# A gated recurrence followed by a gated linear unit on one core: square roots in batches of four chunks, decay constants by a series, and a new hand-written order of all queues

## The chip, the cores and the metric

The kernel runs on one core of a Trainium2 chip. The metric is the device time in microseconds (us) of one launch; a measurement is the median of several runs. Beside the timed runs there is a profile: one execution of the program, taken by the hardware profiler. The engines are named as in the profile: PE (TensorE, matmul), PEld (its weight loads), DVE (VectorE), ACT (ScalarE), POOL (GpSimd), SP (SyncE, which issues nearly all the DMAs).

## The reference

All inputs are float32. `x`, `r_gate` and `i_gate` have the shape 4 x 6336 x 256. The first half is a gated recurrence along the sequence, the second a gated linear unit with a causal convolution of five taps:

```python
log_a = 8.0 * sigmoid(r_gate) * log(clip(sigmoid(a_param), 1e-6, 1 - 1e-6))
a_t   = exp(log_a)
norm  = sqrt(maximum(1.0 - a_t * a_t, 1e-6))
h_t   = a_t * h_(t-1) + norm * sigmoid(i_gate) * x        # y_t = h_t, h = 0 at the start of each sequence
gate  = sigmoid(sum over k < 5 of conv_w[k] * y[t - 4 + k])
out   = (gate * (y @ w_val)) @ w_out
```

## The kernel before

The four sequences are laid end to end as 25,344 time steps. They are cut into 51 windows (`w`, mostly 512 steps) and 28 chunks (`c`): chunks 0 and 1 have 256 steps, chunk 2 has 512, chunks 3 to 25 have 1024 (two windows each), chunk 26 has 512 and chunk 27 has 256. For a window, the three inputs and the output are 512 KB each (256 KB for the windows of 256 steps).

One chunk passes through these steps; each step is a function named by two letters, and the number behind it is the window or the chunk:

- `lr`, `li`, `lx` (line 278): SP issues the loads of `r`, `i` and `x` of a window into rings of four windows each.
- `ta`, `tb` (lines 296 and 299): ACT takes the tanh of half of `r` and `i`, a chunk at a time (a sigmoid is half of 1 + tanh).
- `tr` (343): PE transposes the result for `r`, half of the channels (`h` = 0, 1) at a time, so that channels lie on the partitions. Where GROUPS names two chunks together, one `tr` covers both.
- `ex` (359): ACT takes the exponential with the decay constant `khf` as scale and bias, which gives `a`, into a ring `aring` of 5120 steps, that is five chunks of 1024.
- `sq` (367, POOL) squares `a` into a second ring of the same length, `ering`; `sa` (375) is the same on ACT.
- `rt` (386): ACT takes the square root for a whole batch of chunks (BATCHES). Exp and tanh lie in one of ACT's table sets and the square root in another, so a table load (line 518) is issued wherever the list passes from one kind to the other. Where the chunks of a batch do not lie end to end in the ring, the root is taken in pieces.
- `pp`, `up` (306 and 318, POOL), or `xp` and `uv` (323, PE and 332, DVE): (1 + tanh) times `x`.
- `nt` (401, PE) transposes the roots back, `xg` (408, DVE) multiplies them in, `xt` (417, PE) transposes the product, `sc` (439, DVE) is the scan over time, one half of the channels at a time.
- `cv` (451, PE) is the convolution of a window, `tg` (458, ACT) its tanh, `vl` (466, PE) the product with `w_val`, `gv` (471, DVE) the gating, `ou` (481, PE) the product with `w_out`, `cd` (489, DVE) or `ca` (491, ACT) the copy out of PSUM, and `st` (502, SP) the store.

The string `ORDER` is the order of all this work, written out: one word for each step, with the PSUM banks behind an `@`. The loop at the end of the kernel goes through the words and issues each step's instructions, so that each engine gets, in its own queue, the subsequence of the words that belong to it. An engine works through its queue in order and waits, at the head, for what the instruction needs. Words that stand together in the list run at about the same time: PE's `cv.45`, the first matmuls that the list names behind `rt.9`, start at 265.50 us, and `rt.9` at 265.45 us. Before the loop stand five set-up words, among them `s_kt` (lines 225 to 235), which computes the decay constant `khf` = 4 log(clip(sigmoid(a_param))) on 128 x 2 numbers.

The recurrence ties the rings together: chunk `c + 5` lies where chunk `c` lay in `aring`, so its `ex` waits for `sc` of chunk `c`.

Of the kernel before, what the change touches and what calls it, by code (L numbers as in the profile page):

```python
# [8 lines left out]
P = 128  # L9
CONV_K = 5  # L10
FP32 = mybir.dt.float32
# [7 lines left out]
BATCHES = [[0, 1, 2], [3, 4], [5, 6, 7], [8, 9, 10], [11, 12, 13], [14, 15, 16], [17, 18, 19], [20, 21, 22], [23, 24, 25],  # L19
    [26, 27]]  # L20
# [3 lines left out]
NU = 10  # L24
# [7 lines left out]
GROUPS = [[0], [1], [2], [3, 4], [5, 6], [7, 8], [9, 10], [11], [12], [13, 14], [15, 16], [17, 18], [19, 20], [21], [22],  # L32
# [3 lines left out]
s_ident s_small s_kt s_diag lr.0 ta.0 tr.0.1@0 lr.1 ta.1 lr.2 ta.2 ex.0.1 tr.1.1@1 ex.1.1 tr.1.0@2 tr.2.0@3 ex.1.0  # L36
ex.2.0 tr.0.0@0 tr.2.1@4 lr.3 lr.4 ex.0.0 sq.0.1 sq.0.0 ta.3 lr.5 lr.6 ta.4 sq.2.0 tr.3.1@0,1 li.2 lx.2 tb.2 ex.2.1
li.0 sq.1.0 s_wl.1 tb.0 lx.0 li.1 sq.1.1 ex.3.1 sq.3.1 sq.4.1 lr.7 tb.1 pp.1 tr.3.0@2,3 ex.3.0 sq.4.0 xp.0@4 uv.0 lr.9
lr.10 ta.6 xp.2@0,1 lr.8 sq.3.0 li.4 li.3 ta.5 tb.3 sq.2.1 s_wl.3 lx.1 lx.4 xp.4@2,3 lx.3 rt.0 uv.2 lx.6 li.6 s_wl.2
s_wl.0 lr.13 up.1 li.5 li.8 nt.0@0 xg.0 nt.2@1 nt.1@0 li.7 uv.4 xt.0@5,4 pp.3 up.3 lx.5 lx.7 lr.14 lr.12 rt.1 xg.1  # L40
xg.2 sc.0.1 sc.0.0 nt.3@6,7 xg.3 tb.4 li.10 lx.8 lr.11 li.9 xt.2@0,1 tr.5.0@2,3 xt.1@4,5 ex.5.0 cv.0@6,7 tg.0 sc.1.1
tb.5 li.12 sc.1.0 xt.3@5,4 sc.2.1 cv.1@6,7 tr.5.1@2,3 tg.1 ex.5.1 sc.2.0 cv.2@0,1 xp.7@6,7 sc.3.0 sc.3.1 s_wcast
vl.1@2,3 gv.1 pp.6 pp.5 vl.0@4,5 up.6 lx.10 up.5 pp.8 gv.0 nt.4@2,3 ou.0.0@4 ou.1.0@5 uv.7 tg.2 ta.8 cd.1.0 sq.6.1
lx.9 li.11 cd.0.0 st.1 st.0 ta.7 up.8 tb.6 tr.7.1@0,1 ex.7.1 xg.4 tr.7.0@6,7 ex.7.0 tb.7 lx.11 vl.2@4,5 gv.2 lr.16
lx.12 li.13 xt.4@2,3 sc.4.1 cv.3@0,1 sq.6.0 sq.5.0 sq.5.1 tg.3 vl.3@4,5 xp.9@6,7 sc.4.0 sq.7.1 sq.7.0 rt.2 lr.15 lr.18
gv.3 pp.10 sq.8.1 uv.9 vl.5@0,1 ou.3.0@4,5 ou.2.0@2,3 cd.3.0 cd.2.0 li.14 lr.17 st.3 lx.13 xp.11@6,7 cv.5@2,3 uv.11
tg.5 st.2 up.10 lx.14 li.15 li.16 pp.12 nt.5@6,7 xg.5 tb.8 li.17 up.12 lx.16 li.18 ta.10 gv.5 ta.9 lr.20 cv.6@4,5
nt.6@2,3 xg.6 nt.7@6,7 sq.8.0 xg.7 xt.5@0,1 cv.4@2,3 tg.4 tg.6 sc.5.0 tr.9.0@6,7 ex.9.0 vl.4@2,3 sc.5.1 gv.4
tr.9.1@4,5 ex.9.1 tb.9 pp.13 up.13 lx.17 lx.15 pp.14 up.14 lx.18 ou.5.0@0,1 cd.5.0 ou.4.0@2,3 cd.4.0 st.5 st.4 li.20
lr.19 sq.10.0 sq.9.0 sq.9.1 sq.10.1 xt.6@6,7 sc.6.1 sc.6.0 vl.6@4,5 gv.6 tb.10 li.22 pp.17 pp.15 pp.16 pp.18 cv.7@2,3  # L50
vl.7@0,1 tg.7 rt.3 xt.7@2,3 gv.7 li.21 up.18 up.17 lr.21 lr.22 cv.9@6,7 ou.6.0@4,5 cd.6.0 ou.7.0@0,1 cd.7.0 up.16
cv.10@4,5 tg.10 cv.8@0,1 st.7 li.19 lx.21 sc.7.1 sc.7.0 vl.9@4,5 tg.9 gv.9 st.6 vl.10@6,7 gv.10 ta.11 lr.23 tg.8
nt.8@2,3 xg.8 lx.22 up.15 tb.12 ou.9.0@4,5 cd.9.0 vl.8@0,1 gv.8 nt.9@6,7 tr.11.1@2 pp.22 xg.9 pp.21 up.21 xt.8@4,5
sc.8.0 ta.12 lr.24 li.26 tb.11 pp.20 pp.19 cv.12@0,1 tg.12 tr.12.1@3 ex.11.1 ex.12.1 sq.12.1 ou.8.0@6,7 cd.8.0
cv.11@0,1 tg.11 tr.12.0@4 tr.11.0@2 up.22 ex.11.0 nt.10@6,7 lr.26 lr.25 sc.8.1 vl.11@0,1 gv.11 xt.9@3,2 sc.9.1 li.25
ta.13 ex.12.0 lx.19 sq.11.1 sq.11.0 up.19 ou.11.0@0,1 cd.11.0 cv.14@4,5 li.23 lx.20 st.8 li.24 ta.14 tg.14 tb.14
vl.12@0,1 up.20 sc.9.0 tr.13.0@4,5 ex.13.0 tr.13.1@2,3 xg.10 ou.10.0@6,7 xt.10@4,5 gv.12 ou.12.0@0,1 ex.13.1 cd.10.0
tb.13 cv.13@6,7 tg.13 st.11 st.9 cv.15@2,3 tg.15 sq.13.0 sq.13.1 lx.25 lr.29 sq.12.0 rt.4 lr.28 st.10 pp.26 pp.23
lx.24 lr.27 sc.10.0 cd.12.0 sc.10.1 vl.14@6,7 vl.13@0,1 gv.13 lr.30 sq.14.0 gv.14 vl.15@2,3 gv.15 cv.17@4,5 st.12
# [490 lines left out]
```

## Time and profile before

| what | value |
|---|---|
| timed runs | 294.39 us median (293.57, 294.39, 295.06) |
| profiled execution, span from first to last instruction | 291.5 us |
| median less that span | 2.9 us |
| busy in the span: ACT, DVE, PE, POOL | 275.0, 247.3, 243.8, 233.0 us |
| moved by DMA | 104.35 MB on SP's queue |
| table loads on ACT | 20 (18 on line 518, one each on lines 186 and 234), 1.28 us each |
| first root of batch 0, of batch 2, of batch 9 (the last) | 28.89, 59.62, 265.45 us |
| end of the last matmul, and of the last copy | 287.5, 288.2 us |

No device time is listed for the profiled execution itself: its span is what is known of it, and the timed median lies 2.9 us above it.

Busy time of an engine is not its share of the blame: the span has a start in which little is loaded yet, a long middle in which all engines run at once, and an end in which the inputs are already consumed. The profile is read stage by stage, and the chain of waits says which engine ended last in each.

### The profile page before, as it was taken

The numbers are of one execution on the slowest core, as the hardware profiler recorded it, in microseconds if no ns is written. First come the engines' busy times: TensorE is split into PE (matmuls) and PEld (weight loads), VectorE is DVE, ScalarE is ACT, GpSimd is POOL, SyncE is SP. The second block draws the span as 40 slices with busy tenths as digits, with TensorE's granted clock in tenths as the row PEclk, the third lists the DMA queues.
The fourth block names the chain that finished last, engine by engine and source line by source line (L and its number), as shares of the span: only waits on it lengthen the run. The fifth ranks groups of instructions, "written<-read, shape, count | busy, mean of one in ns | idle before, by whom it ended". The sixth has DMA issues, their size and how long they took to land.

```text
span 291.5 us, 6283 instructions
## 1 busy us (share of the span) xinstructions
PE 243.8 (84%) x2509; PEld 167.6 (57%) x2509; DVE 247.3 (85%) x206; ACT 275.0 (94%) x198; POOL 233.0 (80%) x155
## 2 busy tenths in 40 slices
PE   2281798997986988989888988899889998999993
PEld 1141475455744766567656666657457765767662
DVE  2030589988999999999999999999999999999891
ACT  7799989999999999999999999999999999999563
POOL 1449789999899899999996599998998799976000
PEclk9996789999999999999999999999999999999999
DMA  7999999999999999999999999999999958983354
GB/s 243 356 409 388 386 408 413 338 419 414 408 417 398 388 393 400 386 347 415 412 398 384 409 410 371 411 339 386 408 414 421 413 211 322 338 329 128 147 217 181
DMA packets 29996, 104.75 MB, mean 359 GB/s; under 512 B 3335, under 2 KB 3854, under 8 KB 29966
## 3 DMA queue, kind: packets, MB, share of 16 engines
q1 hardware_dynamic: 29952, 104.35, 92.6%
q8 instruction: 19, 0.31, 0.4%
q14 instruction: 11, 0.09, 0.1%
q10 hardware_dynamic: 14, 0.01, 0.0%
HBM read 78.39 MB, written 25.95 MB: 358 GB/s over the span
## 4 chain that ended last, share of the span: by engine, by line
ACT 39%; PE 18%; DMA 17%; DVE 12%; issue 12%; SPq 1%; ACTq 0%; DVEq 0%
ACT tbring L299 9%; DMA iring<-in_i_gate_dram 8%; DMA rring<-in_r_gate_dram 8%; ACT ering L386 8%; ACT tgring L458 7%; ACT taring L296 6%; DVE yring L439 5%; PE banks L481 5%; PE banks L451 4%; ACT L518 4%; PE banks L466 3%; ACT aring L359 3%; PE banks L401 3%; DVE oring L489 2%; DVE tgring L471 2%
## 5 line engine op out<-in xcount | busy, mean ns | idle before, releaser
L367 POOL TENSOR_TENSOR ering<-aring 128x1024 f32<-128x1024 f32 (+2 forms) x54 | 91.9, 1723 | 21.4 <-ACT aring L359 21.4
L439 DVE TENSOR_TENSOR_SCAN yring<-aring,yring,banks 128x1024 bf16<-128x1024 f32 (+5 forms) x54 | 105.9, 1988 | 1.3 <-PE banks L417 1.2
L318 POOL TENSOR_TENSOR uring<-tbring,xring 128x1024 bf16<-128x1024 bf16 (+1 forms) x45 | 94.5, 2112 | 3.0 <-PE banks L481 1.3
L451 PE MATMUL banks<-yring,diag 64*64 64x512 bf16 (+7 forms) x1080 | 62.2, 361 | 3.0 <-DVE oring L489 1.7
L471 DVE SCALAR_TENSOR_TENSOR tgring<-tgring,banks 128x1024 bf16<-128x1024 bf16 (+1 forms) x51 | 59.1, 1179 | 5.3 <-PE banks L466 3.1
L466 PE MATMUL banks<-yring,wv 128*128 128x512 bf16 (+4 forms) x216 | 49.5, 361 | 8.7 <-ACT tgring L458 4.2
L359 ACT ACTIVATE aring<-banks,khf 128x2048 f32<-128x2048 bf16 (+3 forms) x38 | 54.5, 1485 | 1.1 <-PE banks L343 1.1
L458 ACT ACTIVATE tgring<-banks 128x1024 bf16<-128x1024 f32 (+1 forms) x51 | 50.5, 1014 | 5.1 <-PE banks L481 3.3
L481 PE MATMUL banks<-wo,tgring 128*128 128x256 bf16 x396 | 50.4, 274 | 5.2 <-DVE tgring L471 3.2
L306 POOL TENSOR_SCALAR tbring<-tbring 128x1024 bf16<-128x1024 bf16 (+1 forms) x45 | 45.8, 1030 | 8.3 <-ACT tbring L299 8.3
L481 PEld LDWEIGHTS <-tgring 128*128 128x128 bf16 x396 | 41.7, 114 | 14.8 <-DVE tgring L471 6.6
L296 ACT ACTIVATE taring<-rring 128x2048 bf16<-128x2048 f32 (+2 forms) x28 | 47.5, 1722 | 1.8 <-DMA rring<-in_r_gate_dram 1.8
L299 ACT ACTIVATE tbring<-iring 128x2048 bf16<-128x2048 f32 (+2 forms) x28 | 48.1, 1727 | 0.6 <-DMA iring<-in_i_gate_dram 0.6
L386 ACT ACTIVATE ering<-ering 128x2048 bf16<-128x2048 f32 (+3 forms) x13 | 44.5, 3454 | 0.1
L451 PEld LDWEIGHTS <-diag 64*64 64x64 bf16 x1080 | 29.0, 106 | 26.9 <-issue 11.4
L408 DVE TENSOR_TENSOR uring<-banks,uring 128x2048 bf16<-128x2048 bf16 (+2 forms) x28 | 30.3, 1092 | 14.7 <-PE banks L401 12.3
L489 DVE COPY oring<-banks 128x1024 f32<-128x1024 f32 (+1 forms) x35 | 40.6, 1185 | 0.8 <-PE banks L481 0.4
L343 PE MATMUL banks<-ident_b,taring 128*128 128x128 bf16 x396 | 30.2, 233 | 9.4 <-ACT taring L296 9.0
L466 PEld LDWEIGHTS <-wv 128*128 128x128 bf16 x216 | 19.7, 97 | 29.8 <-issue 14.4
L343 PEld LDWEIGHTS <-taring 128*128 128x128 bf16 x396 | 25.9, 105 | 16.1 <-ACT taring L296 11.5
L401 PE MATMUL banks<-ident,ering 128*128 128x128 f32 x198 | 29.3, 293 | 3.6 <-ACT ering L386 2.5
L401 PEld LDWEIGHTS banks<-ident,ering 128*128 128x128 f32 x198 | 26.3, 206 | 8.9 <-ACT ering L386 2.7
(37 smaller groups left out, 135.7 us busy)
## 6 DMA issues: line engine op xcount, KB each, us to landing
rring<-in_r_gate_dram SPq DMA_DIRECT2D x48, 512.0 KB, 7.5
iring<-in_i_gate_dram SPq DMA_DIRECT2D x48, 512.0 KB, 8.3
xring<-in_x_dram SPq DMA_DIRECT2D x48, 512.0 KB, 7.5
out_dram<-oring SPq DMA_DIRECT2D x48, 512.0 KB, 5.8
rring<-in_r_gate_dram SPq DMA_DIRECT2D x3, 256.0 KB, 3.0
iring<-in_i_gate_dram SPq DMA_DIRECT2D x3, 256.0 KB, 7.4
xring<-in_x_dram SPq DMA_DIRECT2D x3, 256.0 KB, 7.6
out_dram<-oring SPq DMA_DIRECT2D x3, 256.0 KB, 4.1
```

What stands on the lines that cost most here:

```text
L296: nc.scalar.activation(**tangent(c, taring, NTR, rring, NRI))
L299: nc.scalar.activation(**tangent(c, tbring, NTI, iring, NII))
L318: nc.gpsimd.tensor_tensor(out=u, in0=t1, in1=xt, op=ALU.mult)
L367: nc.gpsimd.tensor_tensor(out=e, in0=a, in1=a, op=ALU.mult)
L386: nc.scalar.activation(out=ering[:].bitcast(BF16)[:, 4 * o:4 * o + 2 * n], in_=ering[:, 2 * o:2 * o + 2 * n], func=ACT.Sqrt, scale=-0.25, ...
L401: nc.tensor.transpose(out=bank[:, k:k + P], in_=ering[:, e + q:e + wins[w] // 2:nq], identity=ident[:])
L439: nc.vector.tensor_tensor_scan(out=yring[:, h, col:col + o1 - o0], data0=aring[:, h, a_at[c] + o0:a_at[c] + o1], data1=xT[:, o0:o1], initi ...
L451: nc.tensor.matmul(out=gp[oh * 64:oh * 64 + 64, h, a:b], lhsT=diag[half * 64:half * 64 + 64, h, k, :], rhs=yring[half * 64:half * 64 + 64, ...
L458: nc.scalar.activation(out=tgring[:, w % NTG, :, 0:wins[w]], in_=live.pop(("gp", w))[:, :, 0:wins[w]], func=ACT.Tanh, scale=0.5)
L466: nc.tensor.matmul(out=val[:, m, a:b], lhsT=wv[:, hk, m * P:(m + 1) * P], rhs=yring[:, hk, col:col + b - a], start=(hk == 0), stop=(hk == ...
L471: nc.vector.scalar_tensor_tensor(out=tgring[:, w % NTG, :, 0:wins[w]], in0=tgring[:, w % NTG, :, 0:wins[w]], scalar=1.0, in1=live.pop(("va ...
L481: nc.tensor.matmul(out=ops[:, j * D:(j + 1) * D], lhsT=gv[:, hk, j:wins[w]:J], rhs=wo[:, hk, :], start=(hk == 0), stop=(hk == H - 1))
```

## The change

Five things are different.

1. **Batches.** BATCHES has eight batches in place of ten, most of them of four chunks. `op_rt` now issues one piece of a batch's root at a time (`rt.2.0`, `rt.2.1`), so that other words can stand between the pieces. GROUPS pairs 11 with 12 and 21 with 22.
2. **Decay constants.** `s_kt` had an exponential and a logarithm on ACT, with a table set that holds both loaded at the start (line 186) and the set for exp and tanh loaded behind them (line 234). Now only the set for exp and tanh is loaded; the logarithm is a series of odd powers on DVE, in 16 instructions on 128 x 2 numbers in place of 4.
3. **Transposes of the product.** `op_xt` does one half of the channels; there are 56 words in place of 28, with the same instructions in all.
4. **Order.** All words are put in a new order, with other banks.
5. **Engines.** Some words change their engine.

| words in the list | before | after |
|---|---|---|
| table loads that the list gives (line 518) | 18 | 14 |
| `rt`: pieces | 13 | 11 |
| `ex`, and as many `tr` | 38 (18 of 2048 columns, 10 of 1024, 10 smaller) | 34 (22, 2, 10) |
| `ca` and `cd` | 16 and 35 | 19 and 32 |
| `sa` (chunk.half) | 26.1, 26.0 (512 columns) | 19.1, 24.0 (1024 columns) |
| `xp` and `uv`, windows | 0, 2, 4, 7, 9, 11 | 0, 1, 2, 6, 9 |
| `pp` and `up`, windows | 45 | 46 |

Loads, stores and all other steps are as many as before. The new list has no table load between `rt.0.0` and `rt.1.0`, nor had the old one between `rt.0` and `rt.1`.

```diff
-BATCHES = [[0, 1, 2], [3, 4], [5, 6, 7], [8, 9, 10], [11, 12, 13], [14, 15, 16], [17, 18, 19], [20, 21, 22], [23, 24, 25],
-    [26, 27]]
+BATCHES = [[0, 1, 2], [3, 4], [5, 6, 7, 8], [9, 10, 11, 12], [13, 14, 15, 16], [17, 18, 19, 20], [21, 22, 23, 24], [25,
+    26, 27]]
...
-GROUPS = [[0], [1], [2], [3, 4], [5, 6], [7, 8], [9, 10], [11], [12], [13, 14], [15, 16], [17, 18], [19, 20], [21], [22],
+GROUPS = [[0], [1], [2], [3, 4], [5, 6], [7, 8], [9, 10], [11, 12], [13, 14], [15, 16], [17, 18], [19, 20], [21, 22],
     [23, 24], [25], [26], [27]]
...
-        nc.scalar.preload_act_table_set("natural_log_exp_and_others")
+        nc.scalar.preload_act_table_set("exp_and_others")
...
         def s_kt():
             kps = banks[:, 0]
             nc.tensor.transpose(out=kps[:, 0:H], in_=ap2[0:H, :], identity=ident[0:H, 0:H])
-            nc.scalar.activation(out=ksig[:], in_=kps[:, 0:H], func=ACT.Exp, scale=-1.0)
-            nc.vector.tensor_scalar(out=ksig[:], in0=ksig[:], scalar1=1.0, scalar2=None, op0=ALU.add)
-            nc.vector.reciprocal(out=ksig[:], in_=ksig[:])
-            nc.vector.tensor_scalar(out=ksig[:], in0=ksig[:], scalar1=1e-6, scalar2=1.0 - 1e-6,
+            low, p, z, q = kcol[:, 0], kcol[:, 1], kcol[:, 2], kcol[:, 3]
+            nc.vector.tensor_scalar(out=low, in0=kps[:, 0:H], scalar1=0.0, scalar2=4.0, op0=ALU.min, op1=ALU.mult)
+            nc.vector.scalar_tensor_tensor(out=p, in0=low, scalar=0.5, in1=kps[:, 0:H], op0=ALU.mult, op1=ALU.subtract)
+            nc.scalar.activation(out=p, in_=p, func=ACT.Exp)
+            nc.vector.tensor_scalar(out=z, in0=p, scalar1=2.0, scalar2=None, op0=ALU.add)
+            nc.vector.reciprocal(out=z, in_=z)
+            nc.vector.tensor_tensor(out=z, in0=z, in1=p, op=ALU.mult)
+            nc.vector.tensor_tensor(out=p, in0=z, in1=z, op=ALU.mult)
+            nc.vector.tensor_scalar(out=q, in0=p, scalar1=1.0 / 15, scalar2=None, op0=ALU.mult)
+            for k in (13, 11, 9, 7, 5, 3):
+                nc.vector.scalar_tensor_tensor(out=q, in0=q, scalar=1.0 / k, in1=p, op0=ALU.add, op1=ALU.mult)
+            nc.vector.scalar_tensor_tensor(out=q, in0=q, scalar=1.0, in1=z, op0=ALU.add, op1=ALU.mult)
+            nc.vector.scalar_tensor_tensor(out=q, in0=q, scalar=-8.0, in1=low, op0=ALU.mult, op1=ALU.add)
+            nc.vector.tensor_scalar(out=khf[:], in0=q, scalar1=4.0 * math.log(1e-6), scalar2=4.0 * math.log1p(-1e-6),
                                     op0=ALU.max, op1=ALU.min)
-            nc.scalar.activation(out=ksig[:], in_=ksig[:], func=ACT.Ln)
-            nc.scalar.preload_act_table_set("exp_and_others")
-            nc.vector.tensor_scalar(out=khf[:], in0=ksig[:], scalar1=4.0, scalar2=None, op0=ALU.mult)
...
-        def op_rt(b):
-            cs = BATCHES[b]
+        def op_rt(b, k):
+            cs = root_pieces(b)[k]
...
-        def op_xt(c, *at):
-            for h in range(H):
-                bank = banks[:, at[h]]
+        def op_xt(c, h, at):
+            bank = banks[:, at]
```

The old list begins like this, up to the first roots:

```
s_ident s_small s_kt s_diag lr.0 ta.0 tr.0.1@0 lr.1 ta.1 lr.2 ta.2 ex.0.1 tr.1.1@1 ex.1.1 tr.1.0@2 tr.2.0@3 ex.1.0
ex.2.0 tr.0.0@0 tr.2.1@4 lr.3 lr.4 ex.0.0 sq.0.1 sq.0.0 ta.3 lr.5 lr.6 ta.4 sq.2.0 tr.3.1@0,1 li.2 lx.2 tb.2 ex.2.1
li.0 sq.1.0 s_wl.1 tb.0 lx.0 li.1 sq.1.1 ex.3.1 sq.3.1 sq.4.1 lr.7 tb.1 pp.1 tr.3.0@2,3 ex.3.0 sq.4.0 xp.0@4 uv.0 lr.9
lr.10 ta.6 xp.2@0,1 lr.8 sq.3.0 li.4 li.3 ta.5 tb.3 sq.2.1 s_wl.3 lx.1 lx.4 xp.4@2,3 lx.3 rt.0 uv.2 lx.6 li.6 s_wl.2
```

The new one begins like this:

```
s_ident s_small s_kt s_diag lr.0 lr.1 lr.2 lr.3 li.0 ta.0 ta.1 lr.4 tr.0.0@7 tr.0.1@6 lr.5 tr.1.1@2 ta.2 ex.1.1 lr.6
tr.2.1@4 ex.0.1 tr.2.0@3 li.2 ex.2.1 tr.1.0@0 li.3 ex.0.0 lx.0 ex.2.0 s_wl.1 sq.0.0 tb.0 ex.1.0 li.4 ta.3 lx.1 sq.1.0
li.1 sq.1.1 sq.2.0 ta.4 sq.0.1 sq.2.1 tb.2 lr.9 tr.3.0@2,3 lx.2 lx.3 ex.3.0 lr.8 tr.3.1@0,1 s_wl.3 s_wl.0 ex.3.1 xp.0@3
sq.4.0 xp.1@7 lx.4 uv.0 s_wl.2 tb.3 sq.3.0 xp.2@4,5 tb.1 li.8 sq.4.1 lr.10 uv.1 lr.7 uv.2 li.6 rt.0.0 sq.3.1 lx.5 li.5
li.7 pp.4 nt.0@4 rt.1.0 lx.6 xg.0 pp.3 xt.0.0@6 nt.1@4 xg.1 up.4 xt.1.0@2 xt.0.1@4 nt.2@7 sc.0.1 sc.0.0 xg.2 s_wcast
```

The new list around the roots of its batch 6 (chunks 21 to 24) reads:

```
ou.33.0@4,5 ta.27 li.46 tg.34 cd.31.0 ou.32.0@0,1 sa.24.0 pp.41 cd.33.0 st.31 xt.20.0@2 tb.23 lx.44 cv.35@6,7 sq.23.1
cd.32.0 cv.36@4,5 sc.20.0 tg.35 st.32 sq.24.1 li.45 tg.36 lx.42 vl.34@0,1 st.30 lr.49 up.41 vl.35@4,5 gv.34 rt.6.0
gv.35 pp.44 vl.36@0,1 lx.45 li.47 gv.36 rt.6.1 pp.42 st.33 nt.21@6,7 lr.47 up.44 li.48 xg.21 ou.35.0@0,1 lr.48
ou.34.0@2,3 cd.35.0 xt.21.0@7 pp.43 sc.21.0 tr.27.0@1 xt.21.1@0 up.42 cv.38@4,5 ca.34.0 sc.21.1 up.43 nt.22@2,3 tg.38
```

Two counts in the new list, used below. From the root `rt.2.0` up to the root `rt.6.0`, ACT has 100 instructions: 8 table loads, 16 `ta` and 16 `tb` of 2048 columns and one `ta` of 512, 16 `ex` of 2048 columns, 31 `tg`, 4 `ca`, 2 `sa`, and six pieces of root before `rt.6.0` (two of 4096 columns, two of 8192, one each of 6144 and 2048). From `nt.21` to the end, PE has the transposes of chunks 21 to 27 (`nt` and `xt`: five chunks of 1024, one of 512, one of 256), the last six `tr` (two each of chunks 25, 26 and 27), 13 `cv` and `vl` of 512 columns and one each of 256, and 16 `ou` of 512 columns and one of 256.

More of the change, by code (lines that the diff above doesn't have):

```diff
@@ L1 @@
+import math
 from contextlib import ExitStack
@@ L38 @@
[L38 to L47, printed above, removed]
@@ L98 @@
+sc.27.1 xt.27.0@1 ca.47.0 sc.27.0 vl.49@6,7 gv.49 st.47 ou.48.0@4,5 cv.50@0,1 ca.48.0 tg.50 ou.49.0@6,7 st.48 ca.49.0
+vl.50@2,3 gv.50 st.49 ou.50.0@4 ca.50.0 st.50
 """
```

143 lines of the change are left out of this document (73 added, 70 removed).

## The prediction

> **What bounds the kernel now.** I read the busy times first, then the stretches, then the chain of waits, then the groups. The page's first lines say that no engine stands alone: ACT is busiest, and three others are within a fifth of it.
>
> ```profile
> span 291.5 us, 6283 instructions
> ## 1 busy us (share of the span) xinstructions
> PE 243.8 (84%) x2509; PEld 167.6 (57%) x2509; DVE 247.3 (85%) x206; ACT 275.0 (94%) x198; POOL 233.0 (80%) x155
> ```
>
> The stretches give, for each, its length, the busy time of PE, PEld, DVE, ACT and POOL, the granted clock, DMA share and rate.
>
> ```profile
> 0.00:20.00 20.00, 9.13 (x56) 6.36 (x57) 2.74 (x9) 16.73 (x20) 5.68 (x13) 1.00 0.90 329
> 20.00:40.00 20.00, 10.97 (x69) 7.30 (x68) 7.45 (x13) 17.96 (x10) 16.70 (x16) 0.74 1.03 393
> ...
> 120.00:140.00 20.00, 17.80 (x180) 12.60 (x180) 19.27 (x15) 19.94 (x14) 20.00 (x13) 1.00 1.01 385
> ...
> 220.00:240.00 20.00, 19.09 (x251) 14.03 (x250) 19.35 (x17) 19.99 (x19) 16.70 (x10) 1.00 0.85 342
> 240.00:260.00 20.00, 18.60 (x180) 12.75 (x182) 19.49 (x16) 19.89 (x18) 18.00 (x14) 1.00 0.95 341
> 260.00:280.00 20.00, 19.98 (x212) 13.11 (x205) 19.01 (x15) 15.73 (x17) 6.88 (x5) 1.00 0.43 164
> ```
>
> From 40 to 260 us ACT is full (19.9 of 20) and DVE nearly so; from 260 to 280 PE is full (19.98) and ACT no longer. So ACT sets the pace of the middle and PE that of the end. The chain says where the one hands over:
>
> ```profile
> 241.52 1.28 ACT L518
> 242.81 5.34 ACT ering L386
> 248.19 1.24 PE banks L401 x8
> ...
> 285.64 0.45 PE banks L466 x4
> 286.17 0.70 DVE tgring L471
> 286.92 0.63 PE banks L481 x4
> 287.57 0.59 ACT oring L491
> ```
>
> It passes from the root of chunks 23 to 25 (line 386) to PE's transposes of it at 248, and stays on PE to 287.5. **An earlier end therefore needs PE to be fed earlier, not only less work on ACT.** The last line is the copy; its store ends the span at 291.5, 4.0 after the last matmul's end at 287.5.
>
> **The change part by part.** Prices are from the groups by form:
>
> ```profile
> L359 ACT ACTIVATE aring<-banks,khf 128x2048 f32<-128x2048 bf16 x18 | 36.8, 2085 | 1.1 <-PE banks L343 1.1
> L518 ACT ACT_TABLE_LOAD x18 | 23.1, 1283 | 0.3
> L386 ACT ACTIVATE ering<-ering 128x6144 bf16<-128x6144 f32 x4 | 21.3, 5333 | 0.0
> L386 ACT ACTIVATE ering<-ering 128x4096 bf16<-128x4096 f32 x4 | 14.5, 3616 | 0.0
> L359 ACT ACTIVATE aring<-banks,khf 128x1024 f32<-128x1024 bf16 x10 | 11.9, 1230 | 0.0
> ```
>
> All ACT rows times their counts give 292.1 us for 198 instructions, but ACT was busy for 275.0: neighbours overlap by 17.1/198 = 0.087 us, which I take off each instruction.
>
> ACT in all: four table loads fewer, 4 x 1.28 = -5.1. At the start one load (1.28) and the logarithm (0.20) go: -1.5. `ex`: ten of 1024 columns become two, 18 of 2048 become 22: -8 x 1.23 + 4 x 2.085 = -1.5. Two pieces of root fewer: from 4096 to 6144 columns a root grows by 1.72, so a piece costs 3.62 - 2 x 1.72 = 0.2 beside its columns: -0.4. Three copies more at 1.02: +3.1. Two squares of 1024 columns (about 1.05, as line 296 of that size) for two of 0.62: +0.9. Nine instructions fewer give back 9 x 0.087: +0.8. Sum -3.7. DVE: three copies (1.215 each) and three `uv` instructions (0.735) go: -5.8; twelve tiny ones come at 0.20, early, where DVE is idle. PE: six fp32 matmuls of line 323 go, 6 x 0.58 = -3.5. POOL: +2.9, by the same counting (three windows more at 1.05 + 2.16, two others moved off, sq replaced); it is idle for 58 us and I cost this at nothing; where its cover goes, it is 2.9.
>
> After a table load the next instruction follows at once: 241.52 + 1.28 = 242.80, and the root starts at 242.81. The Trainium skill (ScalarE: Activation LUTs, What ACT_TABLE_LOAD costs) says more: it puts 2.66 us on each switch, the load and a drain. By that the four loads would be worth 10.6 instead of 5.1; this trace shows no drain beside the load, and the sum goes by the row.
>
> These are not the gain. The end follows from the order, in five terms.
>
> (1) *Start of `rt.2.0`.* ACT's work ahead of it, counted in the lists with these prices: old 53.8 for a start at 59.62, so 5.8 idle; new 54.4 (lighter by 1.5 at the start, but two `tg` of 1.04 more stand ahead of the root). The old first roots ran at 28.89 behind `ta.5` and `ta.6` (3.8 us); the new list puts these behind the roots, which can then begin near 25. In the new list the first `ta` need not wait for line 234's load (till 4.75): line 296 gains up to 1.1. Against it, `khf` comes after 16 DVE instructions, not 4. These ran at a pitch of 0.20 (2.63, 2.83, 3.03), so `khf` is there near 5.9, not 3.6; three tangents and PE's transposes (the old exponentials began at 6.75) hide that, and uncovered it costs 2.3. `ta.4` waited for its load until 12.59; `li.0` is now ahead of that load, 256 KB, 0.65 us at the later rate of 0.4 MB per us. So idle time between 3.7 (0.7 before the first load, some 1.5 for the first data, 1.5 for `ta.4`) and 7.0. In SP's queue `lr.9` now stands ahead of `lx.2` and `lx.3` and waits for `ta.4`, until some 14; landing 7.5 later (the median of such loads), they are there at 21.5, and the roots near 25 hide that. I take 4.6, between floor and old row: `rt.2.0` at **59.0**.
>
> (2) *From `rt.2.0` to `rt.6.0`.* 100 ACT instructions: 8 loads 10.3, tangents 62.2, exponentials 33.4, 31 `tg` 32.2, copies 4.1, squares 2.1, roots 28.5 (8192 columns: 5.33 + 1.72 = 7.05). Sum 172.8, less 100 x 0.087: 164.1. The same count on the old list from `rt.2` to `rt.9` gives 206.3 where the trace has 265.45 - 59.62 = 205.8; scaled, **163.7**. This assumes ACT as full as it was.
>
> (3) `rt.6.0` is one chunk, 2048 columns: **1.9**.
>
> (4) *PE from `nt.21` to the end.* `nt.21` needs `rt.6.0`, and PE works in order, so everything behind it comes later: `nt` 6.8, `xt` 6.3, `tr` 2.1, 13.5 `cv` at 1.18, 13.5 `vl` at 0.92, 16.5 `ou` at 1.02 (group rows: 62.2 us / 1080 x 20 is 1.15 for `cv` with its short windows, 1.21 in the chain; 49.5 / 216 x 4; 50.4 / 396 x 8). Sum **60.6**. Old list, same prices, from `rt.8` at 242.81: 44.8, measured 287.5 - 242.8 = 44.7. PE had no slack there, so I allow none.
>
> (5) Last copy and store: **4.0**.
>
> 59.0 + 163.7 + 1.9 + 60.6 + 4.0 = 289.2, which is 2.3 below the span of 291.5. The profiled execution has no other time listed; the median of the timed runs is 2.9 above its span, so I predict 289.2 + 2.9 = **292.1 us**. Four-chunk batches leave PE more work behind the late roots (60.6, with `rt.6.0` 43 us earlier than `rt.9` was): that eats most of what ACT saves.
>
> **Rivals.** *A: transfers bind, no change.* The bytes stay at 104.35 MB. By 174.6 us the new list needs the load for `tb.19`, the 67.1st MB in SP's order; the old run had moved 68.0 MB by then (its rates added up), so the lead is 0.9 MB, 2.2 us. In a root ACT frees no input buffers: the old pause was 5.3 + 2.6 = 7.9 us, and the slices holding one fell from some 410 to about 340 GB/s, 1.2 us of transfer each. The new pause is 7.05 + 2.6 = 9.6, so up to 1.7 us more each, 8.5 over five batches, less 2.5 for two pauses fewer and 2.2 of lead: up to 3.8. Half of that gives about **294**. For it: the DMA share is 1.0 nearly everywhere until 220. Against it: the slices reach 421 GB/s, and ACT waited for transfers for 2.4 us in all.
>
> ```profile
> GB/s 243 356 409 388 386 408 413 338 419 414 408 417 398 388 393 400 386 347 415 412 398 384 409 410 371 411 339 386 408 414 421 413 211 322 338 329 128 147 217 181
> ...
> HBM read 78.39 MB, written 25.95 MB: 358 GB/s over the span
> ```
>
> The Trainium skill (DMA: Bandwidth & Descriptors, Specifications) states a limit of about 358 GB/s of HBM for a core: by that rule this kernel would already stand at its limit and the change be worth nothing, 294.4. Here 40 to 233 us ran at a mean of 397 GB/s, so this trace does not bear the rule out; A's price and chance come from the rows above.
>
> *B: slower, by the five-chunk ring.* Four chunks of a batch and the pairs of `ex` fill five places of `aring`: `ex.11` waits for `sc.7`, `ex.15` for `sc.11`, `ex.19` for `sc.15`, `ex.23` for `sc.19`. DVE's words between `xg.5` and the end of `sc.7.0` are 25.3 us, and from root start to `xg` it is 3.6 + 1.2: 59.0 + 4.8 + 25.3 = 89.1, where ACT by its own work reaches `ex.11.0` at 90.8. Slack 1.7; the other three, in the same way, 1.1, 1.7 and 3.2. Once DVE is later than that, `ex`, `sq` and root follow, and DVE, which waits for that root, is late again. If it falls 3 us behind in each batch, some 1.5 us per batch pass through: 6 us, **298**. Behind the waiting `ex` stand `tg` and `ca`, for which PE and PSUM wait. For it: DVE was busy 97% of 40 to 260. Against it: DVE has 5.8 less to do.
>
> *C: better.* With the floor of (1) and `cv` at 1.15: 292.1 - 0.9 - 0.4 = 290.8. This is the good end of the forecast, not another case.
>
> **How the numbers follow.** The measurement can tell about 0.5% (1.5 us) from no change. Forecast (with C) 0.50; A 0.27; B 0.23. Forecast alone: 290.8 to 292.9. For 8 in 10 the range takes A and most of B: low 290.0 (C less the 0.8 by which the runs scatter), high 298.5. Faster by over 0.5% is below 292.9: 0.50; same 0.27; slower (above 295.9) 0.23.
>
> **What would show it.** Line 518's group x14. First roots near 25, `rt.2.0` near 59, the root of 2048 columns for chunk 21 near 222.7. From there PE 60 us without gaps. If ACT has idle time in front of `ex` (line 359) with DVE or PE as releaser, B is at work; if in front of lines 296 and 299 with DMA, A. I am wrong on the good side only if PE's words behind `nt.21` take less than their old prices, or if ACT idles less than 3.7 us before `rt.2.0`.

## The result, and the profile after

The changed kernel takes 293.36 us (median of 15 runs, 290.32 to 295.81), the kernel before 294.29 us on the same chip (15 runs, 292.64 to 296.56). The ratio is 0.995, with a 95% interval of 0.9927 to 0.9974: faster by half a per cent, only just clear of no change. A second measurement (the control below) gave 292.3 against 294.28, 0.9893 [0.9866, 0.992]. The ratios leave out runs that lie over 1.5% above the fastest of their kernel, so a ratio need not be the quotient of two medians (0.9968 and 0.9933). The two intervals do not overlap, so two measurements of the same kernel differ by 0.6%, some 1.7 us: smaller differences between experiments of different series are not told apart below. The predicted 292.1 is 1.3 us below the first median of the changed kernel and 0.2 below the second. Of the two medians, the forecast's own band (290.8 to 292.9) holds only the second.

The profiled execution of the changed kernel took 290.37 us with a span of 288.6, so 1.8 us lie around the span, not the 2.9 that the prediction took from a median and a span of different executions. By the same 1.8, the profiled execution of the kernel before took about 293.3, some 1.0 below its median. That of the changed kernel is the second shortest of its 15, 3.0 below its median. Spans are compared with spans here (291.5 and 288.6), medians with medians, but the 2.9 us between the two spans are more than the 0.9 between the medians.

The page of the changed kernel, first lines and the rate of the transfers in 40 slices:

```profile
span 288.6 us, 6228 instructions
## 1 busy us (share of the span) xinstructions
PE 242.1 (84%) x2479; PEld 166.3 (58%) x2503; DVE 244.7 (85%) x212; ACT 271.8 (94%) x189; POOL 235.6 (82%) x157
...
GB/s 242 391 401 357 411 409 410 406 386 367 305 414 420 415 415 308 370 416 414 420 414 417 409 415 416 417 416 415 408 307 353 397 400 298 414 178 220 114 182 254
```

The busy times of ACT and POOL moved as priced: ACT -3.2 (priced -3.7), POOL +2.6 (+2.9). DVE and PE moved less: DVE -2.6 (priced -5.8 and +2.4 for twelve tiny instructions, together -3.4), PE -1.7 (-3.5). The rate is flatter than before, up to 420 GB/s, but it has deep dips: 305 and 308 in the slices behind the roots at 61 to 68 and at 99 to 107 us, and 307 from 209 to 216 us.

The groups by form: the table loads, and the roots of the new sizes.

```profile
L369 ACT ACTIVATE aring<-banks,khf 128x2048 f32<-128x2048 bf16 x22 | 44.8, 2069 | 0.9 <-PE banks L353 0.9
...
L532 ACT ACT_TABLE_LOAD x14 | 18.0, 1283 | 0.2
L402 ACT ACTIVATE ering<-ering 128x8192 bf16<-128x8192 f32 x2 | 14.1, 7037 | 0.0
```

Fourteen loads at 1.28; a root of 8192 columns takes 7.04 (priced 7.05); `ex` waits 0.9 us in all, so the five-chunk ring of rival B did not bind in this execution.

The stretches (length, then busy time of PE, PEld, DVE, ACT, POOL, then granted clock, DMA share, rate), first of the kernel before, then of the changed one, between the roots of batch 2 and of the last full batch, and around 160 us:

```profile
59.62:242.81 183.19, 163.75 (x1797) 114.52 (x1796) 178.16 (x139) 182.84 (x121) 169.47 (x103) 1.00 0.99 389
138.00:180.00 42.00, 37.88 (x435) 27.29 (x432) 41.94 (x32) 41.94 (x27) 35.80 (x22) 1.00 1.02 397
```

```profile
61.03:224.16 163.13, 143.92 (x1535) 100.72 (x1549) 157.84 (x121) 162.49 (x100) 156.78 (x95) 1.00 1.00 393
138.00:180.00 42.00, 36.58 (x400) 25.94 (x403) 40.74 (x32) 41.96 (x26) 41.12 (x25) 1.00 1.03 415
```

Before, the first row spans 18 chunks, 183.19 / 18 = 10.18 us per chunk; after, 16 chunks, 163.13 / 16 = 10.20. **The pace of the middle is the same.** This is no sign yet of a limit behind ACT, for ACT's own busy time per chunk is the same too (182.84 / 18 and 162.49 / 16, both 10.16): per chunk, this stretch gives ACT no less to do than before, although the list as a whole has four loads fewer. So the 2.6 us by which the last matmul ends earlier (287.5 to 284.9) come from elsewhere: `rt.2.0` is 1.4 later (59.62 to 61.03); the old kernel took 44.7 us from its last full root to the end of PE for five chunks, and with two more chunks at 10.18 that is 65.1 for seven; the new one takes 60.7 for its last seven (224.16 to 284.9). 1.4 - 4.4 + 16 x 0.02 = -2.7. In these two profiles the gain lies in the end. This is a reckoning from two single executions, not an experiment, and no run below takes the new order of the end alone. In the second rows ACT, POOL, DVE and the transfers stand together: 41.96, 41.12 and 40.74 of 42.00 us, a DMA share of 1.03 at 415 GB/s.

The chain of waits of the changed kernel at the hand-over to the end and in its last five us (start, duration, engine, tile, line):

```profile
222.87 1.28 ACT L532
224.16 7.01 ACT ering L402 x2
231.21 1.02 ACT oring L505
232.28 2.18 PE banks L416 x16
...
255.56 0.82 DVE tgring L485
...
259.05 2.27 DVE yring L453
...
282.98 0.45 PE banks L480 x4
283.52 0.70 DVE tgring L485
284.27 0.62 PE banks L495 x4
284.96 0.59 ACT oring L505
```

The hand-over goes again from the root of the last full batch to PE, 18.7 us earlier (224.16 for 242.81), with more of the work behind it. But it goes through both pieces of that root and a copy on ACT (`ca.34`, whose banks `nt.22` takes): the chain reaches PE at 232.28, not with `nt.21` at 226.12. From there on it lies on PE, but for 255.56 to 261.3, where it lies on DVE (three gatings and a scan), and the last gating at 283.52. No tanh of ACT is on it.

### The profile page after: what moved, and what is told of

The parts are those of the page before. It is cut to its first block, busy times and chain, and to the rows that moved or that the text cites. A ratio compares the mean times of both kernels' runs of the same rounds, so it can differ in the third digit from the quotient of the medians.

```text
span 288.6 us, 6228 instructions
## 1 busy us (share of the span) xinstructions
PE 242.1 (84%) x2479; PEld 166.3 (58%) x2503; DVE 244.7 (85%) x212; ACT 271.8 (94%) x189; POOL 235.6 (82%) x157
## 4 chain that ended last, share of the span: by engine, by line
ACT 33%; PE 25%; DMA 21%; DVE 7%; issue 7%; POOL 4%; SPq 1%; ACTq 0%; DVEq 0%; POOLq 0%
DMA iring<-in_i_gate_dram 10%; ACT ering L402 8%; PE banks L465 7%; DMA rring<-in_r_gate_dram 7%; ACT taring L306 6%; ACT tbring L309 6%; PE banks L495 5%; ACT aring L369 5%; PE banks L480 5%; ACT tgring L472 4%; DMA xring<-in_x_dram 3%; POOL ering L377 3%; PE banks L431 3%; ACT L532 3%; PE banks L416 3%
## 5 line engine op out<-in xcount | busy, mean ns | idle before, releaser
L377 POOL TENSOR_TENSOR ering<-aring 128x1024 f32<-128x1024 f32 (+2 forms) x54 | 90.2, 1687 | 17.3 <-ACT aring L369 17.3
L328 POOL TENSOR_TENSOR uring<-tbring,xring 128x1024 bf16<-128x1024 bf16 (+1 forms) x46 | 97.6, 2136 | 2.1 <-DMA xring<-in_x_dram 1.5
L316 POOL TENSOR_SCALAR tbring<-tbring 128x1024 bf16<-128x1024 bf16 (+1 forms) x46 | 47.2, 1036 | 15.6 <-ACT tbring L309 15.6
L369 ACT ACTIVATE aring<-banks,khf 128x2048 f32<-128x2048 bf16 (+3 forms) x34 | 52.9, 1602 | 1.0 <-PE banks L353 0.9
L480 PE MATMUL banks<-yring,wv 128*128 128x512 bf16 (+4 forms) x192 | 48.4, 359 | 4.5 <-ACT tgring L472 2.1
L465 PEld LDWEIGHTS <-diag 64*64 64x64 bf16 x1080 | 29.9, 107 | 26.6 <-issue 10.8
L402 ACT ACTIVATE ering<-ering 128x2048 bf16<-128x2048 f32 (+4 forms) x11 | 44.2, 4045 | 0.5 <-POOL ering L377 0.4
L503 DVE COPY oring<-banks 128x1024 f32<-128x1024 f32 (+1 forms) x32 | 37.0, 1182 | 2.0 <-PE banks L495 1.3
L416 PE MATMUL banks<-ident,ering 128*128 128x128 f32 x198 | 30.3, 297 | 7.5 <-ACT ering L402 4.4
L431 PE MATMUL banks<-ident,uring 128*128 128x128 f32 x198 | 31.5, 282 | 5.4 <-DVE uring L423 4.0
```

The costliest lines, as they stand in the source:

```text
L328: nc.gpsimd.tensor_tensor(out=u, in0=t1, in1=xt, op=ALU.mult)
L369: nc.scalar.activation(out=dst, in_=src, func=ACT.Exp, scale=khf[:, h:h + 1], bias=khf[:, h:h + 1])
L377: nc.gpsimd.tensor_tensor(out=e, in0=a, in1=a, op=ALU.mult)
L402: nc.scalar.activation(out=ering[:].bitcast(BF16)[:, 4 * o:4 * o + 2 * n], in_=ering[:, 2 * o:2 * o + 2 * n], func=ACT.Sqrt, scale=-0.25, ...
L416: nc.tensor.transpose(out=bank[:, k:k + P], in_=ering[:, e + q:e + wins[w] // 2:nq], identity=ident[:])
L465: nc.tensor.matmul(out=gp[oh * 64:oh * 64 + 64, h, a:b], lhsT=diag[half * 64:half * 64 + 64, h, k, :], rhs=yring[half * 64:half * 64 + 64, ...
```

## The experiments

The theory to test was the prediction's own: ACT sets the pace of the middle, PE that of the end (theory 1). Against it stood that the transfers bind (theory 2), and in the last series that ACT and the transfers both stand at their limit, so that each hides the other (theory 3), or that a third limit lies behind them. The control belongs to the first series (it and the next three experiments); the later ones are compared with the changed kernel through their ratios to the kernel before, which ran beside each.

**Control: the changed kernel once more.**

> The changed kernel once more, as the control of this series: 0.995 of the kernel before within 0.003, some 293.0 us, if the first measurement was no accident of its chip. Both theories need this number only as the base of the others.

292.3 against 294.28, 0.9893 [0.9866, 0.992]. Twelve runs went from 290.61 to 295.32, and the profiled one was the longest, with a span of 293.5. There `rt.2.0` and `rt.3.0` are 41.97 us apart (60.38, 102.35), against 38.59 in the first profile (61.03, 99.62). The chain of waits in that stretch:

```profile
63.91 3.60 ACT ering L402
...
75.12 11.52 DMA rring<-in_r_gate_dram
...
86.75 0.04 ACT taring L306
```

A load of `r` issued at 75.12, behind the root's pause, landed at 86.64, 11.5 us later, and a tangent waited 2.2 us for it. The same program, with the same order, ran without that wait in the other profile. So one later load accounts for 2.2 of the 3.4 us by which these two roots are farther apart. Of the 4.9 us between the two spans, 3.9 lie between `rt.2.0` and `rt.6.0` (167.0 for 163.1) and 1.7 behind `rt.6.0`; the rest of them was not traced.

**The new list with the old decay constants** (`s_kt` as before the change, with its logarithm and two table sets).

> The new list with the old decay constants (logarithm on ACT, two table loads at the start). Theory 1 (a chain of ACT's work up to the root of chunk 21, then PE's work to the end): ACT's first tangent goes back from 3.4 to 4.75, but the tangent of chunk 4 waits for its load at 13.0 in the changed profile anyway (0.6 idle), so of 1.4 us at most 0.6 to 1.0 reach the end: +0.3 to +1.0 us against the control. Theory 2 (transfers bind): the early loads of r are then freed later too, +1.0 to +1.4. If the series were a cost rather than a saving: below 0.

292.09, 0.9944 [0.9917, 0.997]: by medians 0.2 us less than the control, by the ratios 1.5 more, so not told apart from it. The first root began at 25.26 against 24.11 in the first profile of the changed kernel, but kernels that are alike up to there began it anywhere from 24.1 to 25.8. The run is inconclusive for a cost under 1 us.

**Four table loads back, in the middle.**

```diff
+            if word in ("ta.14", "ta.18"):
+                assert have == EXP
+                nc.scalar.preload_act_table_set(SQRT)
+                nc.scalar.preload_act_table_set(EXP)
```

> The new list with four table loads put back in the middle, two ahead of the tangent of chunk 14 and two ahead of that of chunk 18. Theory 1: ACT is on the chain up to the root of chunk 21, so 4 x 1.28 = 5.1 less overlap, +4.5 to +5.1 us against the control, and the span from the root of batch 2 to that of batch 6 grows from 163.1 to 168. Theory 2 (transfers bind from 140 to 215 us, where the rate is flat at 415 GB/s): ACT has slack there, +0 to +3.

299.21, 1.018 [1.0134, 1.0227]: 6.9 us more than the control by medians and 8.4 by the ratios, for 4 x 1.28 = 5.1 us of work on ACT. Theory 1 holds here, and theory 2's +0 to +3 is out. This addition in the middle costs its full price and some more; from `rt.3` to `rt.4` the profile shows 43.13 us for 38.97, from `rt.4` to `rt.5` 45.65 for 42.95, and every row of a load still reads 1283 ns. Where the excess over 5.1 sits is open. The Trainium skill (ScalarE: Activation LUTs, What ACT_TABLE_LOAD costs) puts some 2.66 us on a switch with its drain; four such would be 10.6, an estimate from that figure, and neither this run nor the next reaches that.

**The same four loads, in the end**, where ACT is idle for part of the time.

```diff
+            if word in ("tg.46", "tg.48"):
+                assert have == EXP
+                nc.scalar.preload_act_table_set(SQRT)
+                nc.scalar.preload_act_table_set(EXP)
```

> The new list with four table loads put back behind the last root, two ahead of each of the tanh of windows 46 and 48. Theory 1: PE holds the chain there and ACT sat idle for some 6 us behind 262 us, but the tanh of a window stands between two of PE's steps: +0 to +2 us against the control. If ACT still set the pace at the end: +4.5 to +5.1.

297.25, 1.0096 [1.006, 1.0132]: 5.0 us more than the control by medians, 6.0 by the ratios. **Theory 1's price (0 to +2) fails here**; the measured time is at what was expected if ACT still set the pace at the end. The chain of this run behind the added loads:

```profile
273.29 1.03 ACT tgring L472
274.36 0.38 PE banks L480
...
279.09 1.28 ACT L533
280.38 1.03 ACT tgring L472
281.46 0.38 PE banks L480
```

And its waits from 224 us on (engine and line, waited for, us in total, times, longest):

```profile
PE banks L480 <- ACT tgring L472: 4.6, 3, 2.2
```

PE's `vl` now waits 4.6 us for the tanh of ACT, a wait that the changed kernel does not have in this stretch. From `rt.7.0` to the last matmul it is 4.64 us longer. So the tanh, which is not on the chain of the changed kernel, comes on it when it is held back by two loads (2.57 us). The run does not show that no idle time of ACT is of use in the end: in the changed kernel ACT waits 5.3 us there ahead of its copies, but under 0.1 ahead of `tg.46` and 0.22 ahead of `tg.48`, where the loads were put. Loads ahead of a copy were not tried.

**The old list with the series alone** (the new `s_kt` in the kernel before).

> The old list with the new decay constants alone (one table load and the logarithm off ACT, 16 small instructions on DVE). Theory 1: ACT's first tangents begin some 1.2 us earlier, but the load that the tangent of chunk 4 waits for (until 12.59) is freed by them and comes at most as much earlier, and the exponentials wait for khf until 5.9: -0.3 to -1.0 us against the kernel before (ratio 0.9965 to 0.999). Rival: hidden by the early loads, 0.

293.25 against 294.03, 0.9981 [0.9958, 1.0005]. The interval takes in no change, so no gain is shown. In the one profile the first root begins at 28.13 for 28.89, all later ones 0.6 to 0.8 earlier, and the span is 290.9 for 291.5; this fits the expected -0.3 to -1.0, but the first roots of the executions named above, alike up to there, differ by up to 1.7.

**The old list with two switches less.** The roots of batches 5 and 7 are left out: a square stands in their place, for which the list issues no table load.

```diff
-                                     in_=ering[:, 2 * o:2 * o + 2 * n], func=ACT.Sqrt, scale=-0.25, bias=0.25)
+                                     in_=ering[:, 2 * o:2 * o + 2 * n], func=ACT.Square if b in (5, 7) else ACT.Sqrt,
+                                     scale=-0.25, bias=0.25)
...
-            if table.get(name, have) != have:
+            if table.get(name, have) != have and word not in ("rt.5", "rt.7"):
```

> [...] Theory 1: ACT is on the chain until the root of batch 8, PE works 176 of 183 us between batch 2 and batch 8, so it can take in most of it: -3.0 to -4.8 us (ratio 0.984 to 0.990). Theory 2 (transfers bind): -0 to -2. If four loads fewer with the order kept are worth much more than the whole change (-1.5 us), the new order itself gave the rest away.

292.82 against 294.03, 0.9957 [0.9934, 0.9979]: 1.2 us for four loads of 5.1 us. `rt.8` begins at 241.26 for 242.81. Theory 1's -3.0 to -4.8 is out, and the time lies in theory 2's range, but the rows do not point at the transfers: from 138 to 180 us ACT has 2.0 us free, DVE is busy for 41.98 of 42.00 (41.94 in the kernel before), and two roots wait for POOL's squares (0.46 and 0.76 us). The relief of ACT ran into something else; whether DVE or POOL is not separated.

**The changed kernel with half of the stores.** 38 windows store half of their output, 10 MB less.

```diff
-            nc.sync.dma_start(of[wstart[w]:wstart[w] + n, :].rearrange("(p j) d -> p j d", p=P),
-                              oring[:, w % NOSB, 0:J, :])
+            m = J // 2 if 3 <= w < 41 else J
+            nc.sync.dma_start(of[wstart[w]:wstart[w] + n, :].rearrange("(p j) d -> p j d", p=P)[:, 0:m, :],
+                              oring[:, w % NOSB, 0:m, :])
```

> The new list, storing only half of each window's rows for windows 3 to 40 (10 MB of 104 fewer written; half of these outputs are left out). Theory 1: transfers are not on the chain, -0.5 to +0.5 us against the control (ratio 0.993 to 0.997). Theory 2 (transfers bind in the middle): 10 MB at 415 GB/s are 24 us of transfer, so the lateness that they cause goes, -1 to -4 us.

290.63 against 294.03, 0.989 [0.9869, 0.991]: 1.7 to 2.7 us less than the changed kernel's two medians, but the ratio is that of the control (0.9893), so this run alone does not show that the transfers bind. Its six runs lie close together (290.0 to 291.8).

**The changed kernel without any table load in the list.** All roots are left out, with squares of the same sizes in their place.

```diff
-                                 in_=ering[:, 2 * o:2 * o + 2 * n], func=ACT.Sqrt, scale=-0.25, bias=0.25)
+                                 in_=ering[:, 2 * o:2 * o + 2 * n], func=ACT.Square, scale=-0.25, bias=0.25)
...
-        table, have = {"ta": EXP, "tb": EXP, "tg": EXP, "ex": EXP, "rt": SQRT}, EXP
+        table, have = {"ta": EXP, "tb": EXP, "tg": EXP, "ex": EXP}, EXP
```

> The new list with every root taken as a square, so that all 14 table loads of the list go, 18 us of ACT (the roots are left out). What bounds behind ACT? Theory 1: ACT's part of the chain shortens until DVE (245 busy) and PE (242) bind: from the 8 us before batch 6 that PE and DVE idle in the middle, -6 to -10 us against the control. Theory 2 (transfers bind): -0 to -3, with loads as the last releaser of ACT.

290.02 against 294.03, 0.9872 [0.9849, 0.9896]: 14 x 1.28 = 18 us less on ACT are worth 2.3 to 3.3 us by medians, 0.6 to 2.3 by the ratios (0.9893 and 0.995 without the edit). Theory 1's -6 to -10 is out. From `rt.2.0` to `rt.6.0` it is 161.8 us, 1.3 less, where eight loads (10.3 us) are gone. The stretch:

```profile
138.00:180.00 42.00, 36.77 (x400) 25.85 (x402) 41.40 (x32) 39.89 (x25) 41.76 (x26) 1.00 1.03 415
```

ACT has 2.1 us free, and POOL is at 41.76, DVE at 41.40, the transfers at their rate as before.

**SP's queue in another order.** Forty loads and stores are moved ahead of loads that wait; nothing else changes. An example, around `rt.2.1`:

```
old: cd.5.0 up.10 nt.5@4,5 xg.5 nt.6@6,7 up.11 lx.14 ... up.12 ... li.18 li.17 ta.10 st.3
new: cd.5.0 up.10 lx.14 st.3 nt.5@4,5 xg.5 nt.6@6,7 up.11 lx.15 st.4
```

SP in the changed kernel, from 60 to 80 us (start, duration, what it issues):

```profile
61.56 7.64 SPq L288 DMA_DIRECT2D xring<-in_x_dram  x3
...
72.32 1.03 SPq L516 DMA_DIRECT2D out_dram<-oring  x2
...
79.90 0.34 SPq L516 DMA_DIRECT2D out_dram<-oring  x1
```

The outputs of windows 3, 4 and 5 were ready at 64.4, 65.5 and 66.6 us, but their stores stood behind loads that waited for `up` and for tangents, and left at 72.3, 72.8 and 79.9. From 60 to 74 us the transfers ran at 358 GB/s.

> The new list with 40 words of SP's queue (16 stores, 24 loads) moved ahead of a load that the profile shows waiting for its buffer while they were ready; nothing else changes. In the changed profile the rate falls to 186-290 GB/s at 70 to 76 us, behind the root of batch 2, with stores 3, 4 and 5 ready since 64 to 67 and queued behind a load of x. If transfers are late because of these gaps (and make the spread of the changed kernel's runs, 290.3 to 295.8): -1 to -2.5 us against the changed kernel (ratio 0.985 to 0.991) and a narrower spread. Rival (ACT alone sets the pace, the gaps cost nothing): 0 (0.994), and where the moved stores push loads back, +1.

289.58 against 294.61, 0.9838 [0.9799, 0.9877]. **Of the versions that leave nothing out, this one is the fastest**: 0.6 to 1.1% below the changed kernel, clear of its first measurement (0.995) and at the edge of its second (0.9893), with six runs from 288.75 to 291.61. Its rate:

```profile
span 287.0 us, 6236 instructions
...
GB/s 262 409 405 371 409 407 410 407 410 416 414 414 413 417 407 412 408 410 413 416 350 389 382 419 415 416 419 416 415 416 390 389 417 304 258 78 146 179 121 254
```

The dips to 305 and 308 are gone (the slices there read 414 and 412), and from 60 to 74 us the rate is 413 GB/s for 358; a new dip to 350 stands at 143 to 151 us. So the blocked queue was what lowered the rate there, and since only SP's queue differs, what is gained comes from when the transfers run. This is near rival A's mechanism, but not the same: the loads ahead of the stores waited for `up` on POOL as well as for ACT. Where a median run gains was not seen. In the two single profiles the roots lie equally far apart (163.0 and 163.1 us from `rt.2.0` to `rt.6.0`), and the 1.6 us between their spans arise ahead of `rt.2.0` (59.24 and 61.03).

**Without table loads and with half of the stores**, the two edits above together.

> Both reliefs together: every root a square without table loads (18 us of ACT less) and half of the rows of windows 3 to 40 not stored (10 MB less). Each alone gave some -2 us. Theory 3 (ACT and transfers both stand at their limit, so that each hides the other): together -6 to -10 us against the changed kernel, ratio 0.960 to 0.975. Rival (behind both lies a third limit, DVE at 98% busy or the loop root - transposes - scans - exponential of the five-chunk ring): -2.5 to -4, ratio 0.981 to 0.987, and the roots of batches 4, 5 and 6 stay 42 us apart.

288.34 against 294.61, 0.9785 [0.9735, 0.9836]: between theory 3 and its rival, some 3 to 5 us below the changed kernel by the ratios. The roots of batches 4, 5 and 6 stay 42 us apart (136.43, 179.00, 220.93), as the rival says.

**The same, and half copies.** Also `cd` copies only half of the columns for these 38 windows, 15 us less on DVE.

```diff
+                if 3 <= w < 41:
+                    dst, src = dst[:, 0:wins[w]], src[:, 0:wins[w]]
```

> As the one before, and DVE's copies of windows 3 to 40 take only half of their columns (29 copies of 0.69 in place of 1.215, 15 us of DVE less; the rest is not copied). If DVE is the third limit: the roots of batches 4, 5 and 6 come 39 to 40 us apart in place of 42, and the time falls by another 5 to 12 us. If it is the ring's loop with its waits, or PE: another 0 to 3.

287.45, 0.9745 [0.9705, 0.9785]: 0.9 us less by medians, no clear gain over the one before, and the roots are still 42 us apart (138.02, 180.40, 222.34). So DVE, for which 5 to 12 us were expected, is not the third limit. Two stretches, and what the roots of this kernel waited for:

```profile
138.00:180.00 42.00, 36.35 (x400) 26.17 (x403) 36.75 (x32) 40.20 (x24) 41.91 (x25) 1.00 0.98 375
180.00:222.00 42.00, 39.38 (x419) 27.54 (x423) 39.41 (x34) 39.92 (x27) 39.09 (x25) 1.00 0.83 310
```

```profile
L402 ACT ACTIVATE ering<-ering 128x8192 bf16<-128x8192 f32 x2 | 14.1, 7042 | 1.0 <-POOL ering L377 1.0
L402 ACT ACTIVATE ering<-ering 128x4096 bf16<-128x4096 f32 x3 | 10.8, 3616 | 2.1 <-POOL ering L377 2.1
L402 ACT ACTIVATE ering<-ering 128x6144 bf16<-128x6144 f32 x2 | 10.7, 5339 | 0.9 <-POOL ering L377 0.9
```

With ACT, DVE and the transfers all relieved, POOL is left at 41.91 of 42.00 in the first stretch, and the roots wait for POOL's squares. Batch by batch from `rt.2.0` to `rt.6.0`, POOL is busy for 38.75 of 38.92, 37.33 of 37.41, 42.29 of 42.38 and 39.03 of 41.94 us. It is full in three batches, but not in the fourth: there it waits once itself, 2.8 us for a tangent of ACT (`tb`). What holds the fourth batch at 42 us, the loop through the five-chunk ring for one, is open. POOL's prices, from the changed kernel:

```profile
L377 POOL TENSOR_TENSOR ering<-aring 128x1024 f32<-128x1024 f32 x44 | 82.6, 1892 | 6.5 <-ACT aring L369 6.5
L328 POOL TENSOR_TENSOR uring<-tbring,xring 128x1024 bf16<-128x1024 bf16 x45 | 96.4, 2158 | 2.1 <-DMA xring<-in_x_dram 1.5
...
L316 POOL TENSOR_SCALAR tbring<-tbring 128x1024 bf16<-128x1024 bf16 x45 | 46.6, 1046 | 15.6 <-ACT tbring L309 15.6
```

A chunk takes two of each: 2 x (1.89 + 2.16 + 1.05) = 10.2 us, about the pace of the middle. Between `rt.2.0` and `rt.6.0` the new list moves two squares off POOL (`sa.19.1`, `sa.24.0`), and POOL's busy time there is 156.78 us in the changed kernel, 9.8 per chunk; with the others relieved, it is 157.41 of 160.65. So POOL stands close behind ACT, which is the fuller one in the changed kernel itself (162.49 of 163.13). That POOL bounds the relieved kernel is read from these rows; a kernel with less work on POOL was not tried.

**Less work for PE in the end.** `vl` leaves out half of its sum for windows 38 to 50, 5.6 us less on PE.

```diff
+                    n = 1 if w in range(38, 51) else H
-                    for hk in range(H):
+                    for hk in range(n):
```

> The new list with half of the value product left out for windows 38 to 50 (two matmuls of 512 columns fewer in each, 13 x 0.43 = 5.6 us of PE less, all behind the transposes of chunk 21; those values are then half sums). Theory 1 (PE works without a gap from there to the end): -3 to -5 us against the changed kernel, ratio 0.978 to 0.985. Rival (a chain of latencies through tanh, gating and scans, which four table loads at the end lengthened by 4.6): -0 to -2, ratio 0.988 to 0.995.

291.08 against 294.61, 0.9868 [0.9826, 0.9911], between the two theories and not told apart from the control (0.9893). In the profile it is 59.68 us from `rt.6.0` to the last matmul's end, for 60.72: 1.0 less, though the work left out was priced at 5.6 (PE's busy time shows 2.5 less: 54.15 in 59.00 us, for 56.61 in 58.76). PE holds the chain of the end, but other paths are nearly as long.

## Why the prediction was right, and where not

*The size, right, and in part by luck.* Faster by a little was the likeliest case, and the predicted 292.1 is 1.3 us from the first median. But 293.36 lies between the forecast's own band and rival A's 294, and two errors offset each other: the run at the median has a span of 291.6, which the predicted 289.2 misses by 2.4, and the 2.9 added to it were 1.1 too many. The profiled execution is the second shortest of 15, so the terms below fit it better than they would fit the median one. Term by term, from the first profile of the changed kernel:

| term | predicted | measured |
|---|---|---|
| (1) start of `rt.2.0` | 59.0 | 61.03 |
| (2) `rt.2.0` to `rt.6.0` | 163.7 | 163.1 |
| (3) root of chunk 21 | 1.9 | 2.0 (`nt.21` at 226.12) |
| (4) PE from `nt.21` to the end | 60.6 | 58.8 |
| (5) last copy and store | 4.0 | 3.7 |
| span | 289.2 | 288.6 |
| around the span | 2.9 | 1.8 |

*Term (1)* was 2.0 too early. The first roots were on time (24.11; predicted near 25), and `khf` was there at 5.6 to 5.8 (predicted near 5.9), hidden as said. The stretches up to `rt.2.0`, before and after:

```profile
0.00:59.62 59.62, 37.60 (x289) 24.35 (x289) 29.04 (x36) 54.29 (x42) 41.45 (x38) 0.91 0.98 369
```

```profile
0.00:61.03 61.03, 40.51 (x337) 25.71 (x340) 33.16 (x51) 55.39 (x42) 44.09 (x39) 0.94 0.99 380
```

ACT was busy 55.4 us (counted: 54.4) and idle 5.6 (taken: 4.6), against 54.3 and 5.3 before. So half of the miss is work that the count left out, and half is idle time expected to go: the first `ta` did begin 1.4 us earlier (3.39 for 4.75), but the second, the third and `ta.4` then waited for their loads (0.18, 1.04, 0.62), and `ta.4` began at 13.02, no earlier than the old 12.59. The work moved forward into waits for the same transfers. The upper end of the range for idle time, 7.0, takes this in.

*Term (2)*, the longest, was right to 0.6 in this profile (the control's has 167.0). Counting ACT's own list and scaling by the old run worked here because ACT was full (162.49 of 163.13).

*Terms (3) and (4)* had about the right length by a path that is not quite the one taken. The prices as printed in (4) add up to 60.4, not 60.6. PE was busy 56.6 of the 58.8 us: its words cost some 4 less than priced and it stood still for 2.2. "PE had no slack there, so I allow none" is what failed: the kernel before had 42.4 us of work in its 44.7 too. And the chain does not go from the root of chunk 21 to `nt.21`; it goes on through `rt.6.1` and a copy on ACT to `nt.22` at 232.28. PE had waited only 0.46 us for that copy, so the two paths are nearly equally long. That PE alone sets the pace of the end is too simple: the loads in the end (+5.0) and the lighter `vl` (-1.0 in the profile for 5.6) show that ACT's tanh and other steps are close behind it.

*"ACT sets the pace of the middle"* is borne out for added work: 5.1 us on ACT cost 6.9 or more. For work taken away it is not: 18 us less are worth some 0.6 to 3.3. "It is idle for 58 us and I cost this at nothing" is a step of POOL's price that does not hold: POOL's idle time lies in the start and the end, and in the middle it has 9.8 us of work per chunk at a pace of 10.2. For the predicted time this cost nothing, since ACT was the fuller engine there.

*Rival A* is there in part, smaller than priced. The rate falls behind the roots, and moving the stores gets back 0.6 to 1.1%; but the sign that the prediction named for it, ACT idle ahead of tangents with DMA as the releaser, is absent from the middle of the first profile (2.2 us in all, ahead of 61 us) and stands once in the middle of the control's (2.2 us). It did not bring the time back to 294.4. The limit of 358 GB/s that the Trainium skill (DMA: Bandwidth & Descriptors, Specifications) states for a core did not hold here either: the slices from 123 to 209 us moved 408 to 420 GB/s. *Rival B* is not seen: 0.9 us of idle time before `ex`.

What stays open: which of the five parts of the change makes its half per cent (the series alone gave no clear gain, and the new order and the batches were not taken apart), what a lighter POOL would bring, why the addition in the middle costs more than its length, and which waits make one run of the same program 5 us longer than another beyond the one that the control's profile shows.

## What to carry to other kernels

Where several engines and the transfers are all within a few per cent of full, price what is added to the fullest one in full, and what is taken away only up to the next limit; look for that limit stretch by stretch, by work per unit (here per chunk), and not by idle time in the whole span. Idle time of an engine is of use only where it stands: ask whether it lies ahead of the step that you delay. Read the queue that issues the transfers as one reads an engine: here stores that were ready stood behind loads that waited for busy engines, and the rate fell to 358 GB/s where 413 were possible. And measure the same kernel twice before a difference of half a per cent is given a cause.

## What the runs showed of the hardware

The transfers held 408 to 420 GB/s for 87 us (122.7 to 209.2, twelve slices) beside four busy engines; before the change no stretch of that length did. Every table load took 1283 ns, wherever it stood, and the root behind it began within 0.02 us (222.87 + 1.28 = 224.15, start 224.16). A one-core program of a fixed order spread over 5 us (290.3 to 295.8) from execution to execution; with the stores moved, over 2.9 in six runs. In two profiles of it, one load that landed later makes 2.2 of the 4.9 us between the spans; the rest is not explained, and the granted clock does not order the first 15 runs (0.988 at 290.37 us and at 294.89).
